# The last four groups' second product of a feed-forward layer, from full products to seven half-wide block products

## The chip, the cores and the metric

The kernel runs on one core of a Trainium2 chip (trn2). TensorE (PE) multiplies and loads weights (PEld), VectorE (DVE) and ScalarE (ACT) do elementwise work, GpSimd (POOL) issues indirect transfers, SyncE (SP) issues the other DMAs. The metric is the device time of one execution in microseconds.

## The reference

```python
def reference(q, k, v, g_norm, moe..., moe2...):
    kv = einsum('bhsd,bhse->bhde', k, v);  o = einsum('bhsd,bhde->bhse', q, kv)
    o = o / sqrt(mean(o * o) + 1e-06) * g_norm        # (8, 8, 576, 64)
    x = o.transpose(0, 2, 1, 3).reshape(4608, 512)
    # tokens with x @ w_skip > 0 go to one of 8 experts (512 -> 1024 -> 512, relu), others stay
    x[e] = x[e] + gate * (maximum(x[e] @ w1[e], 0) @ w2[e])
    h = x @ w_in                                       # second feed-forward: (4608, 2048)
    return (h * sigmoid(h)) @ w_out                    # (4608, 512)
```

All is float32. The change lies in the last line, for a part of the tokens.

## The kernel before

Every float32 product is made of three fast ones: each operand is split into a high part (ACT, a copy that rounds) and a low part (DVE, the difference), and PE adds high x high, high x low and low x high. After attention and the experts, the second feed-forward runs over nine groups of 512 tokens, each in four tiles of 128 (`s`). Three groups are *dense*: in 16 steps a step makes 128 hidden columns (`first`) and multiplies the step before's by `w_out` (`second`). The other six groups go in three *pairs*, one `super_group(k)` each, k = 0, 1, 2; here they are called pair one, two and three. A pair's two groups are the two halves of one axis, and its first product is done in seven block products instead of eight (a Strassen-Winograd scheme).

A pair has two stages. The **block stage** calls `block(q)` 56 times: six matmuls of 512 columns each (`pa`, `pb`, `pc` in PSUM), then a sum on DVE and the activation on ACT write a quarter of a hidden tile `g` (`hidden_of(j)`, j = 0 to 7, each with two parts `fi` of the hidden axis for two groups `ni`). The **product stage** runs 32 steps `x`: `prepare(x + LEAD)` makes the two parts `h` of a quarter of `g`, four steps ahead (ACT, then DVE, five buffers `h` in turn), and `product(x)` multiplies it by a part of `w_out`, twelve matmuls of 512 columns into `acc`. All eight PSUM banks hold the eight output tiles; the last step's results are copied out by ACT and DVE in turn and stored (`finish_group`). The last block of the block stage is called after step 0.

The weights of a pair come from DRAM as *entries* of 1 MB into a ring of five tiles (`NWE`): 14 with four blocks each (`weights_a`) and 8 of `w_out` (`weights_b`). `load_entry` asks for the entry five places on when the last product that reads an entry has been issued; SP's queue holds these loads, the stores and everything else it issues in program order. The plain parts are written to DRAM during dense group two (`keep_part`), the sums of the weights of the first product later (`sums_of`).

The next pair's tokens are gathered by POOL (`fetch_pair`, eight calls of four indirect DMAs, held back by `pace`, a copy that waits for a piece of `g`), turned by DVE, summed and split into the seven block operands `b0` to `b6` (`operand_parts`, in the product stage of the pair before). The order is written out by hand: Python generators are stepped once a block or step, and each engine runs its instructions in that order.

## Time and profile before

| | us |
|---|---|
| three runs | 1158.49, 1159.91, 1160.99 |
| median | 1159.91 |
| the profiled execution | 1158.88 |
| its span | 1157.1 |
| PE busy | 1122.7 (97%) |
| DVE busy | 601.7 (52%) |
| ACT busy | 501.8 (43%) |

Three views are read. The table of stages gives the busy time of each engine in a stretch of time. The timeline gives the start of a run of like instructions, the time to the end of its last, and how many there are; the distance between two starts divided by the count is the time that one takes from its neighbours. The chain gives what ended last, step by step.

### The profile page before, as it was taken

How to read it: one execution, taken by the hardware profiler on the slowest of the kernel's cores; microseconds unless marked ns; L12 is line 12 of the kernel's file. 1: busy time of each engine (PE TensorE's matmuls, PEld its weight loads, DVE VectorE, ACT ScalarE, POOL GpSimd, SP SyncE). 2: the span in 40 equal slices, each digit the busy share in tenths (PEclk: the TensorE clock that was granted, in tenths of full speed). 3: DMA queues.
4: the chain of work that ended last, by engine and by line, in shares of the span. 5: the costliest groups of instructions: out<-in, count | busy, mean ns of one | idle time of the engine just before them, and what ended most of it. 6: DMA issues, size and time to landing. Idle time of an engine off the chain costs nothing.

```text
span 1157.1 us, 16746 instructions
## 1 busy us (share of the span) xinstructions
PE 1122.7 (97%) x6283; PEld 934.5 (81%) x6283; DVE 601.7 (52%) x1111; ACT 501.8 (43%) x983; POOL 324.2 (28%) x337
## 2 busy tenths in 40 slices
PE   8994699999999999999999999999999999999998
PEld 7884698888888888788888888888888888888886
DVE  2468578888887599533535422454122554223222
ACT  3675355555554555433333444432344332344221
POOL 3689224323331174150145043200142300000000
PEclk9998799999999999999999999999999999999999
DMA  9996557666666433198351676422666423654202
GB/s 341 365 359 241 192 165 234 215 223 211 220 208 201 153 120 122 45 292 263 122 161 35 205 262 211 162 105 78 227 220 214 140 73 141 219 187 172 89 31 73
DMA packets 65267, 211.07 MB, mean 182 GB/s; under 512 B 9840, under 2 KB 24688, under 8 KB 53024
## 3 DMA queue, kind: packets, MB, share of 16 engines
q1 hardware_dynamic: 55760, 189.44, 46.8%
q0 software_dynamic: 8064, 20.48, 6.0%
q8 instruction: 50, 0.82, 0.3%
q10 hardware_dynamic: 1360, 0.05, 0.1%
q14 instruction: 33, 0.27, 0.1%
HBM read 162.67 MB, written 47.27 MB: 181 GB/s over the span
## 4 chain that ended last, share of the span: by engine, by line
PE 90%; DVE 4%; DMA 3%; ACT 2%; issue 1%; POOL 0%; SPq 0%; DVEq 0%; ACTq 0%
PE acc L1526 23%; PE acc L1383 21%; PE ph L1331 20%; PE pa L1479 11%; PE pc L1479 6%; PE pb L1479 3%; PE po L474 2%; PE kv L442 1%; PE pt L1232 1%; DMA q<-in_q_dram 1%; DMA v<-in_v_dram 1%; DVE x L217 1%; PE busy L1148 1%; PE kv L444 0%; DVE x L199 0%
## 5 line engine op out<-in xcount | busy, mean ns | idle before, releaser
L1383 PE MATMUL acc<-w,h 128*128 128x512 f32 x1128 | 277.3, 392 | 0.5 <-ACT h L1344 0.5
L1526 PE MATMUL acc<-entry,h 128*128 128x512 f32 x1152 | 265.1, 392 | 0.0
L1331 PE MATMUL ph<-xT,w 128*128 128x512 f32 (+7 forms) x1344 | 264.3, 345 | 0.5 <-ACT xT L1243 0.3
L1526 PEld LDWEIGHTS acc<-entry,h 128*128 128x128 f32 x1152 | 216.3, 188 | 47.9
L1331 PEld LDWEIGHTS ph<-xT,w 128*128 128x128 f32 x1344 | 223.7, 188 | 30.2 <-ACT xT L1243 0.5
L1383 PEld LDWEIGHTS acc<-w,h 128*128 128x128 f32 x1128 | 201.0, 181 | 48.0 <-ACT h L1344 1.0
L1022 POOL DMA_INDIRECT x<-xs,qidx x128 | 128.5, 1004 | 110.8 <-DVE room L1294 48.8
L1507 DVE TENSOR_TENSOR h<-g,h 128x512 fp32r<-128x512 f32 x96 | 66.5, 693 | 147.9 <-ACT h L1506 147.9
L1479 PE MATMUL pa<-b,entry 128*128 128x512 f32 x576 | 141.8, 393 | 0.0
L1479 PEld LDWEIGHTS pa<-b,entry 128*128 128x128 f32 x576 | 108.2, 188 | 24.8
L1506 ACT ACTIVATE h<-g 128x512 fp32r<-128x512 f32 x96 | 60.5, 630 | 146.6 <-PE acc L1526 146.6
L188 DVE TENSOR_TENSOR w<-stg_None,w 128x1024 fp32r<-128x1024 f32 x64 | 83.9, 1312 | 17.3 <-ACT w L187 17.1
L1461 ACT ACTIVATE g<-g 128x512 f32<-128x512 f32 x72 | 45.4, 633 | 103.3 <-DVE g L1459 103.3
L1345 DVE TENSOR_TENSOR h<-sg,h 128x512 fp32r<-128x512 f32 x48 | 33.1, 691 | 96.3 <-ACT h L1344 96.3
L222 POOL TENSOR_TENSOR x<-x,x 128x512 f32<-128x512 f32 x32 | 56.1, 1753 | 96.4 <-DVE x L209 96.2
L1343 ACT ACTIVATE sg<-ph 128x512 f32<-128x512 f32 x48 | 28.7, 597 | 111.3 <-PE ph L1331 111.1
L187 ACT ACTIVATE w<-stg_None 128x1024 fp32r<-128x1024 f32 x64 | 67.4, 1054 | 17.6 <-DMA xs<-rows 9.5
L1479 PE MATMUL pc<-b,entry 128*128 128x512 f32 x288 | 74.3, 393 | 0.0
L1337 ACT ACTIVATE h<-ph 128x304 fp32r<-128x304 f32 (+6 forms) x64 | 27.9, 436 | 97.0 <-PE ph L1331 95.2
L1479 PEld LDWEIGHTS pc<-b,entry 128*128 128x128 f32 x288 | 54.1, 188 | 12.4
L1459 DVE TENSOR_TENSOR g<-pc,u 128x512 f32<-128x512 f32 x24 | 16.6, 691 | 73.0 <-PE pc L1479 73.0
L629 POOL TENSOR_TENSOR rows<-rows,grow 128x512 f32<-128x512 f32 x36 | 41.7, 1186 | 31.9 <-ACT rows L487 31.9
(219 smaller groups left out, 1151.9 us busy)
## 6 DMA issues: line engine op xcount, KB each, us to landing
entry<-wa SPq DMA_DIRECT2D x42, 1024.0 KB, 4.9
stg_None<-in_we_dram SPq DMA_DIRECT2D x64, 512.0 KB, 3.9
entry<-wb SPq DMA_DIRECT2D x24, 1024.0 KB, 4.8
stg<-in_wf_dram SPq DMA_DIRECT2D x32, 512.0 KB, 4.1
xs<-rows SPq DMA_DIRECT2D x8, 1032.0 KB, 9.6
wb<-w SPq DMA_DIRECT2D x16, 512.0 KB, 5.0
wa<-parts SPq DMA_DIRECT2D x32, 256.0 KB, 4.1
k<-in_k_dram SPq DMA_DIRECT2D x7, 1024.0 KB, 8.8
```

The lines of the kernel that those rows point to most:

```text
L187: nc.scalar.activation(w[:, 0, :], t.bitcast(F32), AF.Copy)
L188: nc.vector.tensor_tensor(w[:, 1, :], t.bitcast(F32), w[:, 0, :].bitcast(F32), ALU.subtract)
L222: nc.gpsimd.tensor_tensor(x3, x3, x2, ALU.mult)
L629: nc.gpsimd.tensor_tensor(xv, xv, f.to_broadcast([P, HP, 2, D]), ALU.mult)
L1022: nc.gpsimd.indirect_dma_start(out=rows_of[u][s][:, a * XQ:(a + 1) * XQ], out_offset=None, in_=xblocks, in_offset=bass.IndirectOffsetOnAxi ...
L1331: nc.tensor.matmul(ph[:, 0:n], w[:, wi, kk * P:(kk + 1) * P], x[:, xi, 0:n], start=(kk == 0 and a == 0), stop=(kk == KD - 1 and a == 2),)
L1383: nc.tensor.matmul(accs[u, s][0:m], h[:, hi, s * P:s * P + m], w[:, wi, DM:2 * DM], start=(f == 0 and a == 0), stop=(last and a == 2),)
L1461: nc.scalar.activation(g, acc, AF.Silu)
L1479: nc.tensor.matmul(p, w[:, wi, kk], x[:, xi, kk], start=(i in FIRST_IN_BANK and kk == 0 and a == 0), stop=(kk == 1 and a == 2), skip_group ...
L1506: nc.scalar.activation(h[:, 0], g, AF.Copy)
L1507: nc.vector.tensor_tensor(h[:, 1], g, h[:, 0].bitcast(F32), ALU.subtract)
L1526: nc.tensor.matmul(acc[ni, s], h[:, hi, s * P:(s + 1) * P], w[:, wi], start=(j == 0 and fi == 0 and a == 0), stop=(last and a == 2),)
```

## The change

For pairs two and three the second product is done as seven block products too, and the eight quarters of `w_out` and of `g` are combined for it. One block product takes eight steps, `product_second(x)`, of twelve matmuls with 256 columns; 56 steps make a pair's product stage. `SECOND` is the order of the block products and `PLACE` the quarter of `g` that each reads. `third_sum` (in the block stage) and `later_sum` (in the product stage, 24 calls from step 12 on, three in four steps) overwrite quarters of `g` with sums. The results of the block products gather in two PSUM tiles each (`two`), are summed on the way out into `t`, `v` and `z`, and are stored by halves of the columns (`put_half`).

The sums of `w_out` are made once, in pair one's product stage, from the entries that it reads (`sums2_of`, one call for each of the eight), and stored in DRAM (`weights_t`, eight 128 KB stores for each call); a pair's entries for the product are then 14 instead of 8. `weights_b` is one DRAM tile with the two column halves apart, so that pair one's product reads its moving operand in two pieces.

The operands of the next pair are summed in the block stage (`operand_sums`, at blocks 18, 26, 34 and 42), written to DRAM (two stores of 512 KB a tile), read again (`load_sums`) and only split in the product stage (`operand_split`). The gathers come at blocks 3, 7, ... 31 instead of 6, 13, ... 41 and two in the product stage.

```diff
-    weights_b = [tc.dram_tile([P, 2, 2 * DM], F32, name=f"wb{j}") for j in range(KJ)]
+    weights_b = tc.dram_tile([P, KJ, 2, 2 * DM], F32, name="wb")
+    JH = KJ // 2
+    weights_t = {(i, h): tc.dram_tile([P, JH, DM], F32, name=f"wt{i}_{h}") for i in (4, 5, 6, 7) for h in range(2)}
+    tokens_ab = {}
+    SECOND = (1, 4, 2, 6, 5, 7, 3)
+    PLACE = {1: (0, 0), 4: (1, 1), 2: (1, 0), 6: (1, 1), 5: (0, 0), 7: (0, 1), 3: (1, 0)}
+    COLUMNS = {1: (0, 0), 2: (1, 0), 3: (1, 1)}
...
-            nc.sync.dma_start(weights_b[j][:, odd].rearrange("p (o d) -> p o d", o=2), w[:, :, DM:2 * DM])
+            for h in range(2):
+                a = DM + h * EH
+                nc.sync.dma_start(
+                    weights_b[:, j, odd, h * DM:(h + 1) * DM].rearrange("p (o d) -> p o d", o=2), w[:, :, a:a + EH]
+                )
...
+    def sums2_of(j, w):
+        vec = nc.vector
+        even, odd, s12, high = (xp.tile([P, DM], F32, tag="x", name=nm) for nm in ("even", "odd", "s12", "high"))
+        for t, o in ((even, 0), (odd, 1)):
+            wo = w[:, o].bitcast(F32).rearrange("p (h o d) -> p o h d", h=2, o=2)
+            vec.tensor_tensor(t.rearrange("p (h d) -> p h d", h=2), wo[:, 0], wo[:, 1], ALU.add)
...
+        (b11, b12), (b21, b22) = ((t[:, 0:EH], t[:, EH:DM]) for t in (even, odd))
+        t1, t2, t3, t4 = s12[:, 0:EH], s12[:, EH:DM], b11, b12
+        for o, x, y in ((t1, b12, b11), (t2, b22, t1), (t3, b22, b12), (t4, b21, t2)):
+            vec.tensor_tensor(o, x, y, ALU.subtract)
+        yield
+        for hi, t, ab in ((odd, s12, (5, 6)), (high, even, (7, 4))):
+            nc.scalar.activation(hi.bitcast(F32R), t, AF.Copy)
+            vec.tensor_tensor(t.bitcast(F32R), t, hi, ALU.subtract)
+            for h, i in enumerate(ab):
+                e, slot = divmod(j, JH)
+                for o, part_ in enumerate((hi, t)):
+                    nc.sync.dma_start(
+                        weights_t[i, e][:, slot, o * EH:(o + 1) * EH], part_[:, h * EH:(h + 1) * EH]
+                    )
+            if t is s12:
+                yield
...
+    def operand_sums(u, s):
+        vec = nc.vector
+        ab, sums = (stg.tile([P, 2 * DM], I32, tag="stg", name=nm).bitcast(F32) for nm in ("ab", "sums"))
+        ta, tb, t12, t34 = ab[:, 0:DM], ab[:, DM:2 * DM], sums[:, 0:DM], sums[:, DM:2 * DM]
+        for v, t in ((u, ta), (u + 1, tb)):
+            vec.transpose(t.rearrange("p (k a i) -> p a k i", k=KD, a=KQ), x_of(rows_of[v][s]))
...
+        vec.tensor_tensor(t1, b12, b11, ALU.subtract)
+        vec.tensor_tensor(t2, b22, t1, ALU.subtract)
+        yield
+        vec.tensor_tensor(t3, b22, b12, ALU.subtract)
+        vec.tensor_tensor(t4, b21, t2, ALU.subtract)
+        kept_ab, kept_t = (tc.dram_tile([P, 2 * DM], F32, name=f"{nm}{u}_{s}") for nm in ("ab", "st"))
+        nc.sync.dma_start(kept_ab, ab)
+        nc.sync.dma_start(kept_t, sums)
+        tokens_ab[u, s] = kept_ab, kept_t
+        yield
...
+    def load_sums(u, s):
+        kept_ab, kept_t = tokens_ab.pop((u, s))
+        if s % 2 == 0:
+            loaded["b22"] = sgp.tile([P, GN], F32, tag="sg", name="b22")
+        t = [xgp.tile([P, XW], F32, tag="xg", name="sums")[:, 0:DM] for _ in range(3)]
+        b22 = loaded["b22"][:, s % 2 * EH:(s % 2 + 1) * EH]
+        nc.sync.dma_start(t[0], kept_ab[:, 0:DM])
+        nc.sync.dma_start(b22, kept_ab[:, 2 * DM - EH:2 * DM])
+        for i in range(2):
+            nc.sync.dma_start(t[1 + i], kept_t[:, i * DM:(i + 1) * DM])
...
+        for ii in ((0, 1, 2), (4, 5), (6, 3), ()):
+            for i in ii:
+                nc.scalar.activation(at(i, 0), views[i], AF.Copy)
+            for i in old:
+                nc.vector.tensor_tensor(at(i, 1), views[i], at(i, 0).bitcast(F32), ALU.subtract)
+            old = ii
+            if ii:
+                yield
...
-    entries = ([("a", e) for e in range(NEA)] + [("b", j) for j in range(KJ)]) * NSUP
+    entries, entry0 = [], []
+    for k in range(NSUP):
+        entry0.append(len(entries))
+        entries += [("a", e) for e in range(NEA)]
+        entries += [("b", j) for j in range(KJ)] if k == 0 else [("c", (i, h)) for i in SECOND for h in range(2)]
...
+        if kind == "c" and i[0] in COLUMNS:
+            odd, h = COLUMNS[i[0]]
+            src = weights_b[:, i[1] * JH:(i[1] + 1) * JH, odd, h * DM:(h + 1) * DM]
+            nc.sync.dma_start(t.rearrange("p (j d) -> p j d", j=JH), src)
+            return
+        src = weights_b[:, i] if kind == "b" else weights_a[i] if kind == "a" else weights_t[i]
+        nc.sync.dma_start(t, src.rearrange("p a b -> p (a b)"))
...
+            w = ring[e0 + NEA + j][:, fi].rearrange("p (h o d) -> p o h d", h=2, o=2)
...
+                        acc[ni, s].rearrange("p (h d) -> p h d", h=2), h[:, hi, s * P:(s + 1) * P], w[:, wi],
...
+        def third_sum(j):
+            g = hidden_of(j)
+            nc.vector.tensor_tensor(g[:, 0, 1], g[:, 0, 0], g[:, 0, 1], ALU.subtract)
+        def later_sum(n):
+            i, j = divmod(n, KJ)
+            g = hidden_of(j)
+            o, x, y, op = (
+                (g[:, 1, 1], g[:, 1, 1], g[:, 0, 1], ALU.subtract),
+                (g[:, 0, 0], g[:, 1, 1], g[:, 0, 0], ALU.add),
+                (g[:, 1, 0], g[:, 1, 0], g[:, 1, 1], ALU.subtract),
+            )[i]
+            nc.vector.tensor_tensor(o, x, y, op)
...
+            g = hidden_of(j)[(slice(None),) + PLACE[SECOND[i]]]
+            h = ready[x] = next_h()
+            nc.scalar.activation(h[:, 0], g, AF.Copy)
+            nc.vector.tensor_tensor(h[:, 1], g, h[:, 0].bitcast(F32), ALU.subtract)
...
+        def product_second(x):
+            n, j = divmod(x, KJ)
+            i = SECOND[n]
+            if j == 0 and i in (1, 4, 6, 5):
+                two[i] = [
+                    ps_a.tile([P, DM], F32, tag=f"a{m + 2 * (i == 5)}", name="two") if i in (1, 5)
+                    else ps_h.tile([P, GN], F32, tag="h", name="two") if i == 4
+                    else ps_t.tile([P, GN], F32, tag="t", name="two") for m in range(2)
+                ]
+            p = two[{2: 1, 7: 6, 3: 5}.get(i, i)]
...
+            last = j == KJ - 1
+            for s in range(GT):
+                for a, (hi, wi) in enumerate(((0, 0), (0, 1), (1, 0))):
+                    nc.tensor.matmul(
+                        p[s // 2][:, s % 2 * EH:(s % 2 + 1) * EH], h[:, hi, s * P:(s + 1) * P], w[:, wi],
+                        start=(i in (1, 4, 6, 5) and j == 0 and s % 2 == 0 and a == 0), stop=(last and a == 2),
+                        skip_group_check=True,
+                    )
+            if slot == 3:
+                load_entry(e0 + NEA + e + NWE)
+            if not last:
+                return
...
+            if i == 1:
+                for m, t in enumerate(pair_of("t")):
+                    nc.scalar.activation(t, p[m], AF.Copy)
+            elif i == 2:
+                for m in range(2):
+                    o = xgp.tile([P, XW], F32, tag="xg", name="o")[:, 0:DM]
+                    nc.scalar.activation(o, p[m], AF.Copy)
+                    put_half(0, m, o, 0)
+            elif i in (4, 6):
+                for m, t in enumerate(pair_of({4: "v", 6: "z"}[i])):
+                    vec.tensor_tensor(t, p[m], keeps["t"][m], ALU.add)
+            elif i == 5:
+                for m, t in enumerate(keeps["t"]):
+                    vec.tensor_tensor(t, p[m], t, ALU.add)
+            else:
+                for nm, ni, h in ((("z", 0, 1),) if i == 3 else (("v", 1, 0), ("t", 1, 1))):
+                    for m, t in enumerate(keeps.pop(nm)):
+                        vec.tensor_tensor(t, p[m], t, ALU.add)
+                        put_half(ni, m, t, h)
...
         for q in range(NB - 1):
             block(q)
-            j, x = divmod(q, 7)
-            if more_ and j < 6 and x == 6:
-                pace(hidden_of(j)[:, 0, 1])
-                fetch_pair(j // 2, j % 2)
+            for j in new:
+                third_sum(j)
+            i, j = blocks_order[q]
+            new = [j] if i == 1 and k > 0 else []
+            if more_:
+                n, x = divmod(q - 3, 4)
+                if x == 0 and 0 <= n < 2 * GT:
+                    if n:
+                        pace(recent[0])
+                    fetch_pair(n // 2, n % 2)
+                n, x = divmod(q - 18, 8)
+                if x == 0 and 0 <= n < GT:
+                    turning.append(operand_sums(u + 2, n))
+                step_on(turning)
+                if q in (49, 51):
+                    load_sums(u + 2, (q - 49) // 2)
             if q >= NB - 1 - 3 * LEAD and (NB - 1 - q) % 3 == 0:
-                prepare(LEAD - (NB - 1 - q) // 3)
-            yield
-        for x in range(4 * KJ):
-            prepare(x + LEAD)
-            product(x)
+                (prepare_second if k else prepare)(LEAD - (NB - 1 - q) // 3)
+            yield
...
+        SPLIT_AT = {0: 0, 4: 1, 8: 2, 48: 3} if k else {2: 0, 8: 1, 14: 2, 20: 3}
+        for x in range((7 if k else 4) * KJ):
+            if k:
+                if x == 1:
+                    for j in new:
+                        third_sum(j)
+                n0, n1 = (max(0, min(3 * KJ, -(-3 * (y - 12) // 4))) for y in (x, x + 1))
+                for n in range(n0, n1):
+                    later_sum(n)
+                prepare_second(x + LEAD)
+                product_second(x)
+            else:
+                prepare(x + LEAD)
+                product(x)
             if x == 0:
                 block(NB - 1)
             if more_:
-                s, p = divmod(x - 2, 6)
-                if p == 0 and 0 <= s < GT:
-                    room = [xp.tile([P, DM], F32, tag="x", name="room") for _ in range(4)]
-                    queue.append(operand_parts(u + 2, s, room))
+                if x in SPLIT_AT:
+                    queue.append(operand_split(u + 2, SPLIT_AT[x]))
                 if queue and next(queue[0], queue) is queue:
                     queue.pop(0)
-                if x in (5, 6):
-                    fetch_pair(GT - 1, x - 5)
-            yield
+                if x - 4 in SPLIT_AT and SPLIT_AT[x - 4] + 2 < GT:
+                    load_sums(u + 2, SPLIT_AT[x - 4] + 2)
+            if k == 0:
+                if x % 4 == 0:
+                    sums_now.append(sums2_of(x // 4, ring[e0 + NEA + x // 4]))
+                step_on(sums_now)
+            yield
```

On PE, around the last block of pair two's block stage (`pa`, `pb` are its blocks, `entry` the weights). Before:

```order
L1479 MATMUL pb<-b_7533,entry_8458 128x512 x6
L1526 MATMUL acc<-entry_8493,h 128x512 x12
L1479 MATMUL pa<-b_7535,entry_8458 128x512 x6
L1526 MATMUL acc<-entry_8493,h 128x512 x36
L1526 MATMUL acc<-entry_8534,h 128x512 x48
```

and now:

```order
L1595 MATMUL pb<-b_7630,entry_8738 128x512 x6
L1707 MATMUL two<-entry_8782,h 128x256 x12
L1595 MATMUL pa<-b_7632,entry_8738 128x512 x6
L1707 MATMUL two<-entry_8782,h 128x256 x36
L1707 MATMUL two<-entry_8822,h 128x256 x48
```

Behind the same block, runs of twelve with 512 columns have become runs of twelve with 256; from here to the next pair 56 of them stand where 32 stood.

On DVE, in pair two's product stage (`h` is the prepared operand, `g` the hidden tile, `room`, `sums` and `b` belong to the next pair). Before, from step 3 on:

```order
L1507 TENSOR_TENSOR h_8687<-g1_1_8207,h_8687 128x512
L1294 STREAM_TRANSPOSE room_8706<-x15_0_8169 128x4x4x32
L1294 STREAM_TRANSPOSE room_8707<-x16_0_8172 128x4x4x32
L1507 TENSOR_TENSOR h_8719<-g1_1_8207,h_8719 128x512
L1311 TENSOR_TENSOR room_8708<-room_8707,room_8706 128x256
L1312 TENSOR_TENSOR room_8708<-room_8707,room_8708 128x256
L1313 TENSOR_TENSOR room_8709<-room_8707 128x256
L1314 TENSOR_TENSOR room_8709<-room_8706,room_8708 128x256
L1507 TENSOR_TENSOR h_8743<-g1_2_8275,h_8743 128x512
L1308 TENSOR_TENSOR b0_8710<-room_8706,b0_8710 128x2x128
```

and now, at steps 11 to 15:

```order
L1677 TENSOR_TENSOR h_9206<-g1_7_8934,h_9206 128x512
L1411 TENSOR_TENSOR b6_8989<-sums_9073,b6_8989 128x2x128
L1411 TENSOR_TENSOR b3_8986<-sums_9073,b3_8986 128x2x128
L1668 TENSOR_TENSOR g1_0_8369<-g1_0_8369 128x512
L1677 TENSOR_TENSOR h_9226<-g1_0_8369,h_9226 128x512
L1668 TENSOR_TENSOR g1_1_8444<-g1_1_8444 128x512
L1677 TENSOR_TENSOR h_9242<-g1_1_8444,h_9242 128x512
L1668 TENSOR_TENSOR g1_2_8520<-g1_2_8520 128x512
L1677 TENSOR_TENSOR h_9258<-g1_2_8520,h_9258 128x512
L1677 TENSOR_TENSOR h_9273<-g1_3_8608,h_9273 128x512
L1727 TENSOR_TENSOR v_9290<-two_9143,t_9134 128x512
```

Transposes and sums of the next operand have left this stage; beside each low part `h` there now stands a sum over `g`, and from step 15 sums out of PSUM (`v`).

On SP, towards the end of pair two's block stage (`wa`, `wb`, `wt` are weights in DRAM, `ab` and `st` the kept sums). Before:

```order
L1416 DMA entry32_8337<-wa10_88 128x2048
L1416 DMA entry33_8374<-wa11_89 128x2048
L1416 DMA entry34_8414<-wa12_90 128x2048
L1416 DMA entry35_8458<-wa13_91 128x2048
L1416 DMA entry36_8493<-wb0_92 128x2048
L1416 DMA entry37_8534<-wb1_93 128x2048
```

and now:

```order
L1524 DMA entry34_8692<-wa12_90 128x2048
L1524 DMA entry35_8738<-wa13_91 128x2048
L1374 DMA ab15_2_8753<-ab_8725 128x1024
L1375 DMA st15_2_8754<-sums_8726 128x1024
L1521 DMA entry36_8782<-wb_92 128x4x512
L1521 DMA entry37_8822<-wb_92 128x4x512
L1374 DMA ab15_3_8839<-ab_8810 128x1024
L1375 DMA st15_3_8840<-sums_8811 128x1024
L1524 DMA entry38_8872<-wt4_0_93 128x2048
L1387 DMA sums_8893<-ab15_0_8566 128x512
```

Between the loads of entries there now stand the stores of the kept sums and the loads that bring them back.

## Rows read from the trace of the kernel before

**Rows 1.** The page: busy us by engine; PE, its clock, DMA by slice.

```profile
PE 1122.7 (97%) x6283; PEld 934.5 (81%) x6283; DVE 601.7 (52%) x1111; ACT 501.8 (43%) x983; POOL 324.2 (28%) x337
...
PE   8994699999999999999999999999999999999998
...
PEclk9998799999999999999999999999999999999999
...
GB/s 341 365 359 241 192 165 234 215 223 211 220 208 201 153 120 122 45 292 263 122 161 35 205 262 211 162 105 78 227 220 214 140 73 141 219 187 172 89 31 73
```

**Rows 2.** The page: the chain that ended last, by engine.

```profile
PE 90%; DVE 4%; DMA 3%; ACT 2%; issue 1%; POOL 0%; SPq 0%; DVEq 0%; ACTq 0%
```

**Rows 3.** Stages: block, product of pairs one, two, three; columns in the first line.

```profile
core 0: us, PE busy (x) PEld busy (x) DVE busy (x) ACT busy (x) POOL busy (x), PEclk, DMA share, GB/s
655.50:734.50 79.00, 79.00 (x344) 64.27 (x343) 20.73 (x31) 36.67 (x61) 23.90 (x30) 1.00 0.66 227
734.50:821.20 86.70, 86.70 (x380) 71.00 (x379) 41.25 (x83) 28.39 (x60) 7.81 (x8) 1.00 0.33 116
821.20:900.10 78.90, 78.90 (x343) 64.20 (x342) 19.95 (x30) 36.11 (x61) 23.90 (x30) 1.00 0.65 220
900.10:986.50 86.40, 86.40 (x380) 70.98 (x379) 41.25 (x83) 28.40 (x60) 8.72 (x8) 1.00 0.33 116
986.50:1065.40 78.90, 78.90 (x344) 64.29 (x343) 20.10 (x30) 36.11 (x61) 0.00 (x0) 1.00 0.56 200
1065.40:1152.40 87.00, 87.00 (x379) 70.75 (x377) 21.15 (x31) 19.84 (x32) 0.00 (x0) 1.00 0.17 63
```

**Rows 4.** Timeline of PE around step 0: start us, us, instruction, count.

```profile
897.36 2.92 PE L1526 MATMUL acc<-entry,h 128*128 128x512 f32 x12
900.12 1.53 PE L1479 MATMUL pa<-b,entry 128*128 128x512 f32 x6
...
1062.59 2.92 PE L1526 MATMUL acc<-entry,h 128*128 128x512 f32 x12
1065.35 1.56 PE L1479 MATMUL pa<-b,entry 128*128 128x512 f32 x6
```

**Rows 5.** The chain in order of time, from 655 us: start us, us.

```profile
826.95 2.80 PE pa L1479 x12
...
901.65 85.00 PE acc L1526 x372
1066.92 85.60 PE acc L1526 x372
```

**Rows 6.** Timeline of PE in the last expert and a dense group.

```profile
374.41 1.60 PE L1331 MATMUL ph<-xT,w 128*128 128x256 f32 x12
375.85 1.55 PE L1383 MATMUL acc<-w,h 128*128 128x512 f32 x6
377.24 1.58 PE L1331 MATMUL ph<-xT,w 128*128 128x256 f32 x12
378.65 1.55 PE L1383 MATMUL acc<-w,h 128*128 128x512 f32 x6
...
388.09 1.04 PE L1232 MATMUL pt<-ident,sorted 128*128 128x128 f32 x8
388.88 1.63 PE L1383 MATMUL acc<-w,h 128*128 128x512 f32 x6
...
402.62 2.88 PE L1383 MATMUL acc<-w,h 128*128 128x512 f32 x12
405.34 2.88 PE L1331 MATMUL ph<-xT,w 128*128 128x512 f32 x12
```

**Rows 7.** Groups by shape, whole span: busy us, mean ns, idle before.

```profile
L1331 PE MATMUL ph<-xT,w 128*128 128x256 f32 x96 | 12.7, 282 | 0.0
...
L1526 PEld LDWEIGHTS acc<-entry,h 128*128 128x128 f32 x1152 | 216.3, 188 | 47.9
```

**Rows 8.** Groups by shape in the three pairs, 655 us to the end.

```profile
L1507 DVE TENSOR_TENSOR h<-g,h 128x512 fp32r<-128x512 f32 x96 | 66.5, 693 | 147.9 <-ACT h L1506 147.9
L1308 DVE TENSOR_TENSOR b<-room,b 128x256 fp32r<-128x256 f32 x56 | 20.1, 418 | 0.0
...
L1294 DVE STREAM_TRANSPOSE room<-x 128x512 f32<-128x512 f32 x16 | 10.4, 687 | 0.0
...
L1506 ACT ACTIVATE h<-g 128x512 fp32r<-128x512 f32 x96 | 60.5, 630 | 146.6 <-PE acc L1526 146.6
...
L1304 ACT ACTIVATE b<-room 128x256 fp32r<-128x256 f32 x56 | 18.7, 402 | 0.0
...
L1022 POOL DMA_INDIRECT x<-xs,qidx x64 | 62.2, 972 | 70.4 <-DVE room L1294 48.8 <-issue 19.8 <-DMA entry<-wa 1.1
```

**Rows 9.** Timeline of DVE: two runs of splits in pair one.

```profile
745.78 1.09 DVE L1308 TENSOR_TENSOR b<-room,b 128x256 fp32r<-128x256 f32 x3
...
748.57 1.46 DVE L1308 TENSOR_TENSOR b<-room,b 128x256 fp32r<-128x256 f32 x4
```

**Rows 10.** The page: DMA issues, count, KB each, us to landing.

```profile
entry<-wa SPq DMA_DIRECT2D x42, 1024.0 KB, 4.9
```

**Rows 11.** Waits of SP's queue from 655 us: total us, times, longest.

```profile
SPq L1416 <- PE acc L1526: 180.8, 19, 10.7
```

**Rows 12.** Timeline of the end: a load's issue, the last copy, the last stores.

```profile
1097.50 0.32 SPq L1416 DMA_DIRECT2D entry<-wb  x1
...
1152.54 0.69 DVE L1356 COPY o<-acc 128x512 f32<-128x512 f32 x1 [0.67 <-PE acc L1526]
1153.26 1.11 SPq L1371 DMA_DIRECT2D out_dram<-o  x2
```

More of the change, by code (lines that the diff above doesn't have):

```diff
@@ new lines, in operand_split, with at @@
+    def operand_split(u, s):
+        if s == 0:
+            operand_tiles()
+        src = loaded.pop((u, s))
+        def at(i, o):
+            return operands[i][:, o, :, s * P:(s + 1) * P]
+        views = {i: x.rearrange("p (k n) -> p k n", k=2) for i, x in src.items()}
+        old = ()
+        for ii in ((0, 1, 2), (4, 5), (6, 3), ()):
[6 more added lines that the diff above has]
+                yield
@@ L1370, in finish_group @@
                 t0 = (2 * bp + h) * S + SM
-                nc.sync.dma_start(out[t0:t0 + SR, :], o[h * SR:(h + 1) * SR, :])
+                nc.sync.dma_start(out[t0:t0 + SR, a:z], o[h * SR:(h + 1) * SR, :])
     def second(u, f, c, h):
@@ L1429, in next_h, with step_on @@
         return stg.tile([P, 2 * DM], I32, tag="stg", name="h").bitcast(F32R).rearrange("p (o n) -> p o n", o=2)
+    def step_on(queue):
+        if queue and next(queue[0], queue) is queue:
+            queue.pop(0)
     def super_group(k):
@@ L1581, in tile_kernel @@
     hs = {}
-    sums_now = []
     parts = []
     rooms = []
-    def step_on(queue):
-        if queue and next(queue[0], queue) is queue:
-            queue.pop(0)
     for n in range(len(steps) + LAG):
```

48 lines of the change are left out of this document (40 added, 8 removed).

## The prediction

> **What bounds the kernel now.** First the page: PE is busy 97% of the span and in nearly all of the 40 slices, with its clock at 9 tenths or more in all but two of them [rows 1], and the chain that ended last is 90% PE [rows 2]. So I ask which engine could take PE's place in the part that is edited. The table by stages answers [rows 3]. From 655 us on there are three pairs of groups, each with a block stage (56 block products of six matmuls) and a product stage (32 steps of twelve matmuls). In all six PE is busy without a gap at granted clock 1.00 (2.4 GHz), while DVE is busy 20 to 41 us of 79 to 87, ACT 20 to 37, and the DMA engines 17 to 66%. PE's queue never runs dry there, so the time of a stage is the number of its matmuls times the distance between their starts. That distance I take from starts, not from busy time, because neighbours overlap.
>
> **Removed: the second product of pairs two and three.** Pair two: twelve matmuls from 897.36 to 900.12 (2.76 us) and 372 that hold the chain for 85.00 us, together 87.8. Pair three: 2.76 and 85.60, together 88.4 [rows 4, 5]. Sum 176.1 us.
>
> **Added in its place.** Seven block products of eight steps are 56 steps of twelve matmuls, with 256 columns instead of 512. This shape stands in the trace: the last expert's first product has bursts of twelve 128x256 matmuls on the same kind of operands, between bursts of six with 512 columns. Twelve narrow ones take 374.41 to 375.85 and 377.24 to 378.65, that is 1.44 and 1.41 us; six wide ones between them take 1.39 [rows 6]. I take 1.425 us a step: 56 x 1.425 = 79.8 us a pair, 159.6 for two. **Gain 176.1 - 159.6 = 16.5 us.** The ends: 1.41 a step gives 157.9 (gain 18.2), 1.44 gives 161.3 (gain 14.8). A much worse end is the busy time of the 96 narrow ones, 12.7 us, or 132 ns each [rows 7]; it counts the run-on of every burst, so I don't take it, but it is a rival below. Narrower does not keep paying: eight matmuls of 128 columns begin at 388.09 and the next burst at 388.88, about 100 ns each [rows 6], against 118 for 256 columns, so 256 lies just above a floor that has little to do with columns.
>
> Here a rule speaks. The Trainium skill ("TensorE: Matmul & The Clock Gate", section "LDWEIGHTS (loading the stationary operand)") puts a load of 128 columns at 128/1.2 = 107 ns, whatever the matmul's width, which speaks against halving widths; its section "Back-to-back issue gap" gives 262 cycles for 256 columns, 109 ns at 2.4 GHz. By those figures, as an estimate, two pairs would take 147 us and the time would be 1131. The trace has about 119 and decides.
>
> **DVE and ACT in pair two** (the tightest place). A step now lasts 1.43 us, before 2.7. Each step needs one high part on ACT (0.63) and one low part on DVE (0.69) of the next operand; twenty-four later sums and twelve sums out of PSUM cost 0.69 each on DVE, a split of 256 columns 0.40 on ACT and 0.42 on DVE, seven for each of four tiles [rows 8]. Steps 0 to 11: 12 x 0.69 + 21 x 0.42 + 0.69 = 17.8 us on DVE against 12 x 1.43 + 1.4 (the last block) = 18.5 on PE; where splits follow each other they take 1.09 for three and 1.46 for four [rows 9], which makes it 16.6. Steps 12 to 43: 1.75 x 0.69 = 1.21 a step, with six PSUM sums 42.8 us against 45.6. ACT: 12 x 0.63 + 21 x 0.40 = 16.0 of 18.5. All under PE's time, and operands are made four steps (5.7 us) ahead, while one takes 0.63 + 0.69 once its buffer is free. I put 0 here, and no gain, since none of it shortens PE's work. What is late next if the cover fails: PE's matmuls of the next step. Bound: if DVE loses 0.3 us a step to waits for ACT while it is this full, 1.51 stands against 1.43 for 32 steps (2.6 us) and the first twelve steps end 2 late (16.6 + 3.6 against 18.5): 4.6 us. Pair three has no splits, and DVE work of 56 x 0.69 + 24 x 0.69 + 12 x 0.69 = 63 us of 80.
>
> **DVE and ACT elsewhere.** Transposes and sums of the next operands move from the product stages into the block stages of pairs one and two: 4 x (2 x 0.69 + 4 x 0.42) = 12.2 us onto a DVE that is busy 20 of 79 [rows 3, 8], with 5.5 for the eight third sums of pairs two and three. Pair one's product stage gains, for each of eight weight tiles, 4 x 0.69 + 4 x 0.42 = 4.4 us on DVE, 35.5 in all, and 10 on ACT: DVE goes from 41 to about 65 of 87 with the move taken off, in steps of 2.7 us. Hidden. The gathers on POOL come at every fourth block (5.6 us) instead of every seventh; four of them at 0.97 and about 0.3 of issue are 5.1 [rows 8], and the first sums wait for them only at block 18. Hidden.
>
> **DMA and SP's queue.** A block stage that also fetches moved 220 GB/s at a share of 0.65, so all engines busy would be about 338 [rows 3]. Pairs one and two add there 4.2 MB of kept sums, 1.8 of reloads, 0.5 of gathers: 6.5 MB in 79 us, 303 GB/s, a share of 0.90; between blocks 18 and 46 nearly 1. Product stages rise to about 230 (pair one, 8.4 MB of weight sums in 64 stores), 221 and 150. Cover: an entry of weights is asked for when its slot is freed, four entries ahead (4 x 5.6 = 22 us), and lands in 4.9 [rows 10]; SP waits for PE at these loads, 181 us in the largest of four groups [rows 11], so it has time to issue. 17 us of lateness are free. A store waits for DVE in SP's queue with the next entries behind it, some 3 us, inside those 17. The keeping of plain weights in dense group two takes 16 more stores, about 0.32 us of SP each [rows 12], 5 us over a group of 87: 0.
>
> **Small terms.** Pair one's product now reads its moving operand in two pieces. No row shows that; equal-width matmuls differ from 227 ns (twelve in 2.72 in a dense group [rows 6]) to 230 (372 in 85.60) and 233 (twelve of a block stage in 2.80) [rows 5], so I bound it by -1 and +1.5 and take +0.5. The end: today a copy of 0.69 and two stores follow the last matmul, 4.6 us to the end [rows 12]; then a sum of 0.69 and two half-wide stores. +0.3, between -0.3 and +0.7.
>
> **Sum.** The profiled execution took 1158.9 us (span 1157.1 and 1.8 around it): 1158.9 - 16.5 + 0.5 + 0.3 = 1143.2. The median of three runs lies 1.0 above it, so 1144.
>
> **Rivals.** (a) *DVE late in pair two*: worked out above, 4.6 us, with the other small ends up to 8: 1147 to 1152. For it: 90 to 95% of DVE's time is planned away over 44 steps, with work that waits for PSUM in order. Against: four steps of lead.
> (b) *No fixed part at all*: if a narrow matmul cost half of the dense group's 227, 113 ns, two pairs would take 152 and the time would be about 1137. Against: the narrow bursts themselves [rows 6]. The Trainium skill's figures above go this way and further.
> (c) *Weight loads show*: at the 132 ns of busy time a pair takes 672 x 0.132 = 88.7, hardly more than before, and the time is 1160 to 1162: the change does nothing. A weight load takes 188 ns [rows 7] and hides only behind its neighbours; from 131 ns a matmul nothing is gained. Against: the bursts of twelve hid it [rows 6].
> (d) *Slower, by DMA in the block stages of pairs one and two*: if stores, gathers and loads together got no more than today's 220 GB/s, 23.9 MB would take 109 us, less the stage's 79 and the 17 of cover 12 us each, 24 in all: 1168. It decides from about 230 GB/s downwards. Against: 292 and over 340 stand in slices of this trace [rows 1].
>
> **How the numbers follow.** Forecast 1141 to 1147: 0.66. (a) 0.19, (b) 0.06, (c) 0.04, (d) 0.05. Likeliest time 1144. For eight in ten I take in (a) up to 1151 and the fringe of (b) from 1140.5; (c), (d) and the rest of (b) stay outside. A measurement tells about 0.2% (2.3 us) from no change: faster 0.91, same 0.04, slower 0.05.
>
> **What would show it.** Right: 1344 narrow matmuls about 119 ns apart, PE without gaps through pairs two and three at 1.00, product stages of some 80 us, block stages still 79, the DMA share near 0.9 there. Wrong: idle time of PE ended by DVE or ACT between steps 0 and 48 of pair two (a), by an entry's DMA (d); narrow matmuls over 125 ns apart (c); a product stage of pair one over 88 us (the two-piece read).

## The result and the profile after

The changed kernel took 1146.24 us (median of four, 1142.78 to 1147.48) against 1159.22 us: 0.9877, with a 95% interval of 0.986 to 0.9893, 13 us faster. The profiled execution is the fastest of the four, 1142.78 us, span 1141.0. On two more chips the ratio was 0.9853 (0.983 to 0.9875) and 0.9889 (0.9869 to 0.9909).

The two traces, stage by stage, from the start of each stage's first matmul (for pair one the first behind the last dense product, since two of its blocks run earlier; the last row from the start of the last matmul):

| stage | before, us | after, us | difference |
|---|---|---|---|
| up to pair one | 658.22 | 657.80 | -0.42 |
| block stage, pair one | 73.53 | 73.53 | 0.00 |
| product stage, pair one | 89.44 | 89.44 | 0.00 |
| block stage, pair two | 76.16 | 78.02 | +1.86 |
| product stage, pair two | 89.13 | 80.65 | -8.48 |
| block stage, pair three | 76.10 | 76.28 | +0.18 |
| product stage, pair three | 89.52 | 80.44 | -9.08 |
| from the last matmul on | 4.97 | 4.86 | -0.11 |
| span | 1157.1 | 1141.0 | -16.1 |

The page of the changed kernel (busy us by engine, then slices), beside [rows 1]:

```profile
PE 1104.5 (97%) x6859; PEld 947.4 (83%) x6859; DVE 712.9 (62%) x1303; ACT 537.8 (47%) x1047; POOL 327.1 (29%) x339
...
PEclk9998799999999999999999999999999999999999
DMA  9996657666666534087541479859789875755561
```

PE holds 97% as before, and DVE has 111 us more work. The table of stages, beside [rows 3] (block, product of pairs one, two, three):

```profile
core 0: us, PE busy (x) PEld busy (x) DVE busy (x) ACT busy (x) POOL busy (x), PEclk, DMA share, GB/s
657.80:731.30 73.50, 73.50 (x319) 59.78 (x318) 29.13 (x51) 33.23 (x56) 28.14 (x35) 1.00 0.89 301
731.30:820.80 89.50, 89.50 (x392) 73.28 (x391) 62.55 (x125) 37.67 (x78) 0.47 (x1) 1.00 0.73 229
820.80:898.80 78.00, 76.61 (x332) 61.79 (x331) 33.88 (x59) 34.59 (x59) 32.37 (x39) 1.00 0.91 304
898.80:979.40 80.60, 80.60 (x679) 80.34 (x678) 66.09 (x119) 44.51 (x87) 0.00 (x0) 1.00 0.72 233
979.40:1055.70 76.30, 76.30 (x332) 62.07 (x331) 23.49 (x36) 33.98 (x57) 0.00 (x0) 1.00 0.60 205
1055.70:1136.30 80.60, 80.60 (x679) 80.25 (x677) 57.68 (x91) 36.67 (x59) 0.00 (x0) 1.00 0.48 151
```

Five of the six stages have PE busy for every moment at granted clock 1.00 (2.4 GHz; 0.50 is 1.2 GHz). The block stage of pair two has not: 76.61 of 78.00. The timeline of PE at its end (start us, us):

```profile
893.16 1.65 PE L1595 MATMUL pa<-b,entry 128*128 128x512 f32 x6 [1.39 <-DVE g L1573]
...
898.79 1.59 PE L1707 MATMUL two<-entry,h 128*128 128x256 f32 x12
900.22 1.55 PE L1595 MATMUL pa<-b,entry 128*128 128x512 f32 x6
```

The chain, in order of time:

```profile
882.76 8.37 DMA ab<-ab
891.12 0.02 issue
891.15 0.64 ACT h L1676
...
891.81 0.45 DVE h L1677
...
901.77 77.83 PE two L1707 x660
```

Two things are in these rows. The narrow matmuls, 660 in 77.83 us, are 117.9 ns apart, and step 0 takes 900.22 - 898.79 = 1.43. And PE's gap (1.39 of the 1.86 us; the rest lies in the matmuls next to it, as the six behind it, 1.65 for 1.40) is followed back through DVE and ACT to a *store*: the kept sums `ab`, issued at 882.76 and landed 8.37 us later. The timelines of ACT and of DVE show who waited (in brackets the idle time before and what ended it). ACT:

```profile
891.15 0.63 ACT L1676 ACTIVATE h<-g 128x512 fp32r<-128x512 f32 x1 [3.96 <-DMA ab<-ab]
```

DVE, behind it:

```profile
891.81 0.69 DVE L1677 TENSOR_TENSOR h<-g,h 128x512 fp32r<-128x512 f32 x1 [5.77 <-ACT h L1676]
892.42 0.68 DVE L1573 TENSOR_TENSOR g<-pa,p 128x512 f32<-128x512 f32 x1
```

The prepared operand `h` goes in turn to two buffers of its own and three of a pool (`stg`) from which `operand_sums` now takes `ab` and `sums` too. The high part of `h` could not be written until the store had read `ab` out. ACT and DVE work in order: the sum that empties `pa` stood behind the low part of `h`, and PE needed the PSUM bank.

### The profile page after: what moved, and what is told of

It is laid out like the page before. It is cut to its first block, busy times and chain, and to the rows that moved or that the text cites. A ratio compares the mean times of both kernels' runs of the same rounds, so it can differ in the third digit from the quotient of the medians.

```text
span 1141.0 us, 18526 instructions
## 1 busy us (share of the span) xinstructions
PE 1104.5 (97%) x6859; PEld 947.4 (83%) x6859; DVE 712.9 (62%) x1303; ACT 537.8 (47%) x1047; POOL 327.1 (29%) x339
## 4 chain that ended last, share of the span: by engine, by line
PE 90%; POOL 3%; DMA 2%; DVE 2%; ACT 1%; issue 1%; SPq 0%; DVEq 0%; ACTq 0%
PE acc L1481 22%; PE ph L1424 20%; PE two L1707 14%; PE pa L1595 11%; PE acc L1642 8%; PE pc L1595 6%; PE pb L1595 3%; POOL rows L664 3%; PE po L509 2%; PE kv L477 1%; PE pt L1267 1%; DMA ab<-ab 1%; DVE x L252 1%; PE kv L479 1%; PE G L498 1%
## 5 line engine op out<-in xcount | busy, mean ns | idle before, releaser
L1707 PEld LDWEIGHTS two<-entry,h 128*128 128x128 f32 x1344 | 159.0, 190 | 0.3
L1707 PE MATMUL two<-entry,h 128*128 128x256 f32 x1344 | 159.1, 281 | 0.0
L1677 DVE TENSOR_TENSOR h<-g,h 128x512 fp32r<-128x512 f32 x112 | 77.0, 691 | 42.6 <-ACT h L1676 40.0
L1676 ACT ACTIVATE h<-g 128x512 fp32r<-128x512 f32 x112 | 70.5, 630 | 68.5 <-PE two L1707 53.1
L1642 PE MATMUL acc<-entry,h 128*128 128x512 f32 x384 | 88.4, 392 | 0.0
L1642 PEld LDWEIGHTS acc<-entry,h 128*128 128x128 f32 x384 | 72.1, 188 | 15.9
```

The costliest lines, as they stand in the source:

```text
L1642: nc.tensor.matmul(acc[ni, s].rearrange("p (h d) -> p h d", h=2), h[:, hi, s * P:(s + 1) * P], w[:, wi], start=(j == 0 and fi == 0 and a = ...
L1676: nc.scalar.activation(h[:, 0], g, AF.Copy)
L1677: nc.vector.tensor_tensor(h[:, 1], g, h[:, 0].bitcast(F32), ALU.subtract)
L1707: nc.tensor.matmul(p[s // 2][:, s % 2 * EH:(s % 2 + 1) * EH], h[:, hi, s * P:(s + 1) * P], w[:, wi], start=(i in (1, 4, 6, 5) and j == 0 a ...
```

## The experiments

Four runs (the first runs with DVE's low part repeated on half and on all steps, the first with three copies, and the quarters) fell on a chip on which the kernel before took 1187.16 us and every kernel lost time in places far from its edit, for a cause that I could not find; of those runs only stretches without such stalls are read, and two of the kernels were run again elsewhere.

### The stall at h: one line

```diff
         recent = [None]
+        hr_n[0] = 0
```

`hr_n` counts the buffers of `h`. Set to zero at the start of a pair, it gives the first two prepared operands of a block stage the buffers of their own; the shared three are then needed some six blocks later. No transfer changes.

The changed kernel again:

> The changed kernel again, for its spread and a second profile. Its profiled run took 1142.8 us, its other three 1145.6 to 1147.5. Theory (h buffer): in a pair's block stage the kept sums (ab, st) and the prepared operand h take turns in the same three buffers, so ACT has to wait for a store to be read out before it can write h; in the profile that wait was 3.96 us and cost PE 1.8 us at 893, and it is longer in the slower runs. Then most runs here take 1145 to 1147.5, and if the new profile falls on such a run, the idle time of PE at the end of pair two's block stage is 3 to 6 us, or one of the same kind stands in pair one (at 730), and the rest of the span agrees within 0.5 us. Rival (clock): the slower runs have the same waits, and the clock that was granted is lower over some stretch, with matmuls in it at over twice their distance. Rival (spread of its own): the runs scatter around 1145 as those of the kernel before scatter, by 2.5 us, with no place in the trace.

With the line:

> The changed kernel with one line added: the count that picks the buffer of h starts at zero in every pair, so that the first two prepared operands go to two buffers of their own and the three that are shared with the kept sums are needed at blocks 49, 52 and 55 and not from 43 on. Transfers, their number and their order stay as they are. Theory (h buffer): the idle time of PE at the end of pair two's block stage (1.8 us in the profile) goes, ACT waits under 1 us for ab or st, and the time is 1140.5 to 1142 in nearly every run, 0.995 to 0.998 of the changed kernel, with a spread under 2 us. Rival (transfers at their limit, share 0.91): the stall stays or moves to an entry of weights, and the time is that of the changed kernel within 0.1%. Rival (clock or scatter): the profiled stall goes, 1.8 us, but the spread of 4 to 5 us stays.

Measured on one chip: changed 1143.64 (1143.03 to 1146.69), with the line 1142.54 (1141.49 to 1147.28); ratios to before 0.9853 (0.983 to 0.9875) and 0.9854 (0.9827 to 0.9882). The medians don't separate them; the traces do. The block stage of pair two took 77.83 us without the line and 76.16 with it, as in the kernel before, and PE has no gap. ACT's timeline there, with the line, has `h` without a wait:

```profile
888.31 0.62 ACT L1677 ACTIVATE h<-g 128x512 fp32r<-128x512 f32 x1
```

The table of that stage, with the line:

```profile
822.30:898.46 76.16, 76.16 (x331) 61.96 (x330) 34.01 (x59) 34.72 (x59) 32.38 (x39) 1.00 0.91 304
```

The DMA share is the same 0.91 as with the stall. So the cause is the shared buffer, and not transfers at their limit. But the theory's second half fell: the spread stayed. The profile of the changed kernel here was its slowest run, 1146.69, with the same gap as the fast one (1.7 us of that stage, not the 3 to 6 expected of a slower run). Its span is 3.9 us longer than that of the 1142.78 run, and 4.1 us were there when pair one began (661.89 against 657.80). 3.3 of them were there by 16 us; the table from 10 to 20 us, of the 1142.78 run:

```profile
10.00:20.00 10.00, 7.10 (x102) 5.95 (x101) 0.55 (x1) 3.20 (x10) 0.00 (x0) 1.00 0.98 383
```

Of this one:

```profile
10.00:20.00 10.00, 6.92 (x84) 5.92 (x82) 0.00 (x0) 1.04 (x3) 0.00 (x0) 0.66 0.98 370
```

PE waited 2.7 us for `v` of attention there, against 1.0, and its granted clock was 0.66 against 1.00. The edit isn't near. That the start makes the scatter is shown for this one run only.

Both kernels once more, on a third chip:

> The changed kernel once more beside the one with h's buffers in the new order, for the ratio of the two on another chip. On the chip of the first pair the changed kernel's block stage of pair two lost 1.7 to 1.8 us at one place (893 to 897) and the runs scattered by 4 us over the first 15 us of the span, where the inputs of attention land. Theory: the same here, block stage of pair two 77.6 to 78.0, pairs' product stages 79.2; the time 1143 to 1147. Rival (the stall at h belongs to that chip): 75.9.

> The changed kernel with h's buffers in the new order, again beside the changed kernel. Theory: block stage of pair two 75.9 and everything after it the same to 0.1 us, the median 1.5 to 2 us under that of the changed kernel, within the scatter of the start. Rival (the gain was chance): medians within 0.5 us.

Measured: 1147.18 (1143.28 to 1150.25; 0.9889, 0.9869 to 0.9909) and 1143.25 (1142.07 to 1144.64; 0.9851, 0.9834 to 0.9868). Block stage of pair two: 77.88 with ACT's wait of 4.13 us for `ab`, and 76.16 without. The profiled spans differ by 1.2 us (1141.5 and 1140.3): this stage makes 1.7, and the start 0.4 the other way. The median's 3.9 us are more than the trace explains. The version with the line is the fastest of this study.

### The price of width

The kernel before, with second products in halves, and then in quarters (4 for 2, `P` for `EH`):

```diff
-                for a, (hi, wi) in enumerate(((0, 0), (0, 1), (1, 0))):
+                for z in range(2):
+                    for a, (hi, wi) in enumerate(((0, 0), (0, 1), (1, 0))):
...
-                        acc[ni, s], h[:, hi, s * P:(s + 1) * P], w[:, wi],
+                        acc[ni, s][:, z * EH:(z + 1) * EH], h[:, hi, s * P:(s + 1) * P],
+                        w[:, wi, z * EH:(z + 1) * EH],
...
```

> The kernel before, with every second product of the three pairs issued as 256-column halves: 24 matmuls a step in place of 12, with the same columns, the same products and no other change (768 narrow ones a pair in place of 384 wide). It measures the price of width alone. Theory (118 to 119 ns for a narrow one, 230 for a wide one): a pair's product takes 768 x 0.1185 = 91.0 in place of 88.3 us, 2.7 more a pair, 8 in all: 1166 to 1168. Rival (no fixed part, 113 to 115 ns): 768 x 0.114 = 87.6, 0 to -2 in all: 1157 to 1160. Rival (weight loads show, 132 ns): 768 x 0.132 = 101.4, 39 in all: 1198. Rival (the operand does not change from half to half... it does here, each half loads its three operands again; if a repeated order of high, high, low is what hides the loads, 118 stays).

Measured: 1168.8 us (1166.28 to 1171.10), 1.0072 of before (1.0047 to 1.0098), some 9 us longer. Pair one in the chain:

```profile
734.28 2.87 PE acc L1527 x24
...
738.56 87.83 PE acc L1527 x744
```

744 in 87.83 us are 118.05 ns each, and the pair's product stage took 92.10 us for 89.44. The three product stages lost 2.66, 2.80 and 2.18 us, 7.6 in all, so the theory's 8 holds; 2.4 more stood ahead of pair one. The same columns in halves cost 3% more, so what the change gains comes from the multiplications saved (56 x 12 x 256 columns for 32 x 12 x 512, an eighth less), and 3% of the stage goes back for the width.

> The kernel before with every second product of the pairs issued as 128-column quarters, 48 matmuls a step (1536 a pair). With halves a narrow one took 118 ns in the long run (744 in 87.8 us) against 229 for a wide one. Theory (a floor of about 100 ns a matmul that columns do not lower, as eight of 128 columns showed in 0.79 us): 1536 x 0.100 = 154 us a pair, +64, 192 in all: about 1350. Rival (a fixed part of some 7 to 11 ns beside the columns, no floor): 1536 x 0.062 = 95 a pair, +6: 1178. Rival (weight loads of 188 ns of busy time show in full): 289 a pair, +200: 1760.

Measured: 1711.34 us, far above the theory, and near the last rival's 1760 for another reason than the rival's. The table of stretches, three of pair one's product and one of pair three's, shows two prices:

```profile
755.00:770.00 15.00, 15.00 (x130) 14.72 (x129) 4.49 (x8) 3.50 (x6) 0.50 (x1) 1.00 0.22 74
770.00:800.00 30.00, 28.12 (x169) 27.77 (x169) 5.86 (x14) 4.12 (x11) 7.19 (x8) 0.69 0.17 53
800.00:900.00 100.00, 100.00 (x471) 100.00 (x471) 14.56 (x29) 9.29 (x20) 0.00 (x0) 0.50 0.06 22
...
1539.00:1600.00 61.00, 61.00 (x549) 61.00 (x547) 8.31 (x12) 7.95 (x13) 0.00 (x0) 1.00 0.16 57
```

At granted clock 1.00 one takes 61.00 / 549 = 111 ns, at 0.50 (1.2 GHz) 100 / 471 = 212. So in this stream there is a floor, at 111 and not at 100, and 118 for 256 columns lies 6% above it; pair three, at 1.00 throughout, took 172.8 us for 89.5, 83 more where the theory had 64. The Trainium skill ("TensorE: Matmul & The Clock Gate", section "LDWEIGHTS (loading the stationary operand)") puts a load at its columns divided by 1.2, 107 ns for 128 columns, and 111 agrees with that to 4%. That the loads make the floor is not shown. That the clock fell to half in pairs one and two I had not foreseen, and it makes the larger part of the miss. In pair one PE was busy without a pause for 16 us at 1.00, then paused four times for 0.2 to 0.8 us (in pair two three times for 0.4 to 0.8), and from there to the end of the stage it stood at 0.50, though it was busy all the time; in pair three, without the pauses, it stayed at 1.00. Pauses alone are not enough: the product stages with 256 columns of the run with every low part made twice (below) stood at 1.00 through 50 waits of PE of up to 1.7 us. What else is needed is open, and so is whether that chip had a part in it: the quarters ran on no other.

### The cover of the transfers

An unused copy inside DRAM at each of the eight sums of operands, with the one line above; then three.

```diff
         nc.sync.dma_start(kept_ab, ab)
         nc.sync.dma_start(kept_t, sums)
+        nc.sync.dma_start(tc.dram_tile([P, 4, DM], F32, name=f"more{u}_{s}"), weights_a[s])
```

> The kernel with h's buffers in the new order, and one unused copy of 1 MB inside DRAM (from the kept weights to a scratch tile) at each of the eight sums of the next operands: 4 MB read and 4 MB written more in the block stages of pairs one and two, where the DMA share is 0.86 to 0.91. It measures the cover of the transfers, which the prediction put at 17 us a stage, and the rival that transfers bind. At some 340 GB/s with all engines busy a stage of 79 us can move 26.9 MB; it would have 24 + 4 (a copy counted once) or + 8 (counted twice). Theory (cover of 17 us): 28 to 32 MB need 82 to 94 us, 3 to 15 late, inside the cover but for what h and the reloads wait: 0 to 4 us a stage, 1140 to 1149. Rival (no cover: what is late shows): 3 to 15 us a stage, 1147 to 1171, with PE idle for entries in pairs one and two.

Measured: 1144.13 us (1143.81 to 1146.55), 0.9861 (0.9834 to 0.9888), against 1142.54 without the copies on that chip. The profiled runs differ by 1.8 us, of which 1.5 stand ahead of pair one and 0.3 in pair two's product stage. The two block stages:

```profile
660.00:735.00 75.00, 75.00 (x326) 60.99 (x325) 30.13 (x54) 33.73 (x56) 28.16 (x35) 1.00 0.93 332
824.00:900.00 76.00, 76.00 (x331) 61.80 (x330) 34.13 (x59) 34.54 (x58) 32.80 (x39) 1.00 0.96 339
```

339 GB/s at a share of 0.96, and PE has no gap: what didn't fit went into the product stage (257 GB/s for 238 in pair two). The cover is there, and rival (d) is far off.

> The kernel with h's buffers in the new order and three unused 1 MB copies inside DRAM at each of the eight sums of the next operands (12.6 MB a pair, counted once, in pairs one and two). With one copy each, the block stages moved 332 and 339 GB/s at shares of 0.93 and 0.96, and PE had no gap: what did not fit moved into the product stage. Theory (the prediction's cover of some 17 us, at 340 GB/s): 24 + 12.6 = 36.6 MB a stage need 108 us, 29 late against 17 of cover: 8 to 16 us a pair, with PE idle for entries from about block 44 on or early in the product stage; 1157 to 1173. Rival (cover is larger, since copies queue behind one another on their own and entries share the engines with them rather than wait behind them): 0 to 4 a pair, 1141 to 1149. Rival (no cover): 29 a pair, 1199.

> The run with three unused 1 MB copies at each sum of operands again: its first run fell on a chip where the kernel before took 1187 us and all kernels lost time at places that have nothing to do with the copies, so that its block stages can't be read. Theory (cover of some 17 us at 340 GB/s): 36.6 MB need 108 us, 29 late, 8 to 16 us a pair. Rival (entries share the engines with the copies and the cover is larger): 0 to 4 a pair, 1141 to 1149. In the first run only 2.6 us of PE's waits were put down to an entry, which speaks for the rival.

The first of these took 1220.09 us on the chip of 1187.16, and its block stages aren't read; its product stages, 96.9 and 94.3 us, agree with the second's 96.6 and 94.7. The second took 1190.58 us: 11.4 and 7.1 us more than the kernel with the line in pair one's two stages, 10.9 and 14.2 in pair two's. That is 18.5 and 25.1 a pair, above the theory's 8 to 16, far above the one rival's 4 and under the other's 29. But the theory named the wrong cover. Waits of PE (total us, times, longest):

```profile
PE pa L1598 <- ACT t L1571: 10.6, 4, 5.6
PE acc L1645 <- DVE g L1576: 4.9, 1, 4.9
PE pa L1598 <- DVE g L1576: 4.7, 1, 4.7
PE pc L1598 <- DMA entry<-wa: 4.2, 2, 2.7
PE two L1710 <- ACT h L1679: 3.5, 1, 3.5
```

Waits of DVE:

```profile
DVE sums L1368 <- DMA ab<-ab: 27.8, 4, 10.5
```

The page's landings (count, KB, median us):

```profile
entry<-wa SPq DMA_DIRECT2D x42, 1024.0 KB, 5.9
ab<-ab SPq DMA_DIRECT2D x8, 512.0 KB, 17.6
```

PE waited 28 us in all, and the ring of entries lost 4.2 of them. What ran out first were the three shared buffers: their stores landed after 17.6 us (8.6 in the changed kernel), DVE waited 27.8 us for room for the next sums, and PE waited for the ACT and DVE work behind that. ACT's splits waited another 15.8 us for the reloads (`sums<-ab`). The other 15 of the 43.6 us stand in stages whose granted clock was 0.93 to 0.96, where the kernel with the line had 1.00.

### How near DVE is to its limit

The low part of `h` made twice in pairs two and three, on even steps or on all, with the one line above:

```diff
-            nc.vector.tensor_tensor(h[:, 1], g, h[:, 0].bitcast(F32), ALU.subtract)
+            for _ in range(1 + (x % 2 == 0)):
+                nc.vector.tensor_tensor(h[:, 1], g, h[:, 0].bitcast(F32), ALU.subtract)
```

> The kernel with h's buffers in the new order, and on every second step of pairs two and three DVE makes the low part of h twice (the same result again). It asks how near DVE is to becoming the bound there. In the trace of the changed kernel DVE's operations on 512 columns are busy for 0.69 us but start 0.60 apart when nothing holds them. Theory (spacing counts): steps 12 to 43 need 1.75 x 0.60 + 0.11 for sums out of PSUM = 1.16 us of DVE a step, with the half repeat 1.46, against 1.42 of PE: 1.3 us late after 32 steps, inside the four steps of lead. So 0 to 0.5 us a pair, product stages of 79 to 80, as without it. Rival (busy time counts, as the prediction's bound for a late DVE had it): 1.75 x 0.69 + 0.13 + 0.345 = 1.68 a step, 8.4 us late after 32 steps, less 4 to 5 of lead: 3 to 5 us a pair, product stages of 82 to 84.

> The run with DVE's low part made twice on every second step again, for pair two, whose block stage was disturbed in the first run: its product stage took 82.0 us, pair three's 79.6, against 79.2 and 79.2 without the repeats. A repeat took 0.73 us there, since it writes the same tile as the operation ahead of it. Theory (pair two is nearer to DVE's limit by its splits in steps 0 to 11 and has no lead left at step 12): 81 to 82 again in pair two, 79.4 to 79.7 in pair three. Rival (the disturbed start of that stage): 79.3 to 79.7 in both.

The first run gave 1195.53 us on the chip of 1187.16, the second 1153.36. The expectations mix two ways of counting; counted alike, the 660 matmuls behind the last block took 82.0 us in pair two and 78.1 in pair three in both runs, against 77.7 and 77.8 without repeats. So pair two's 4.3 us do not come from that chip. They lie in the first rival's 3 to 5 and not in the theory's 0 to 0.5; pair three's 0.35, for 0.72 us more of DVE in every two steps, fits the theory alone. What the two pairs differ by are the splits: in the second run DVE was busy for 22.5 of the first 24.4 us of pair two's product stage and for 19.8 of pair three's, and in pair two PE's waits for `h` begin right behind these 24.4 us.

> The same with the low part made twice on every step of pairs two and three. Theory (spacing counts): 1.16 + 0.60 = 1.76 us of DVE a step against 1.42 of PE, 11 us late after 32 steps, less 4 to 5 of lead: 6 to 8 us a pair, product stages of 85 to 88, with PE waiting for h by DVE from about step 25 on; in pair two 2 to 4 more for the splits of steps 0 to 11 (17 spaced operations more). Rival (busy time counts): 2.03 a step, 19.6 late, less 5: 15 us a pair, 95. Rival (DVE's work is hidden in any case, since PE's queue is long): 0, 79.

Measured 1229.73 us on the chip of 1187.16; the product stages, free of its stalls, took 103.6 and 94.9 us, 23.1 and 14.3 more than without repeats: far more than the theory's 8 to 12 and 6 to 8, and in pair three near the rival's 15. A part of the reason is in the timeline of DVE; first the changed kernel (start, us to the end of the last, count):

```profile
919.88 0.69 DVE L1668 TENSOR_TENSOR g<-g 128x512 f32<-128x512 f32 x1
920.48 0.69 DVE L1677 TENSOR_TENSOR h<-g,h 128x512 fp32r<-128x512 f32 x1
921.08 0.69 DVE L1668 TENSOR_TENSOR g<-g 128x512 f32<-128x512 f32 x1
```

With the repeats:

```profile
1150.49 1.41 DVE L1679 TENSOR_TENSOR h<-g,h 128x512 fp32r<-128x512 f32 x2
1151.82 0.68 DVE L1669 TENSOR_TENSOR g<-g 128x512 f32<-128x512 f32 x1
```

Operations on different tiles start 0.60 apart though each is busy for 0.69; the repeat, on the tile just written, starts 1.41 - 0.69 = 0.72 after the first. With it a step needs 1.16 + 0.72 = 1.88 us of DVE against 1.42, which makes 15 over 32 steps. I had priced the repeat too low. But less the 4 to 5 of lead that is 10 to 11, and what makes the rest of pair three's 14.3 is open. So the totals don't tell the theory from the rival; the steps do. Two that PE waited for in pair three:

```profile
1165.46 1.68 PE L1709 MATMUL two<-entry,h 128*128 128x256 f32 x12 [0.25 <-DVE h L1679]
1167.39 1.69 PE L1709 MATMUL two<-entry,h 128*128 128x256 f32 x12 [0.25 <-DVE h L1679]
```

They start 1.93 apart, which is DVE's spacing of a low part, its repeat and a sum, 0.60 + 0.72 + 0.61; three times 0.69 would be 2.07.

## Why the prediction was right, and where it was not

**What bounds the kernel.** Right: PE without gaps at 1.00 in five of six stages, so number times distance was the time.

**Narrow steps.** Right, a little dear: 1.425 us a step forecast from two bursts, 1.415 measured (117.9 ns). The two product stages together lost 17.6 us for 16.5. (b) and (c) are out: without waits the sustained runs at 256 columns stand 117.7 to 118.1 ns apart, not 113 and not 132. The Trainium skill's 262 cycles ("TensorE: Matmul & The Clock Gate", section "Back-to-back issue gap"), as an estimate 109 ns at 2.4 GHz, are given there for an isolated gap and lie 8% under the trace's 118.

**Two-piece read.** +0.5 taken, 0.00 measured; the chain before and after:

```profile
736.06 85.30 PE acc L1526 x372
735.63 85.30 PE acc L1642 x372
```

The 89.44 us of this product stage are not the prediction's sign of a dear read (over 88): they are counted from step 0 on and were the same before. **The end.** +0.3 taken, -0.11 measured.

**DVE in pair two, rival (a).** 0 taken, and no wait of PE for DVE stands in the product stages. My pricing by 0.69 us an operation was too dear: DVE was busy for 15.4 us in the time of steps 0 to 11 and 40.3 in that of steps 12 to 43, where I had 16.6 to 17.8 and 42.8. The bound was not: in the repeats some 0.36 us a step more cost pair two 4.3 us, near the 4.6 that I had put on 0.3 a step, and pair three 0.35. So in pair two rival (a) was less than one operation every other step away.

**DMA, rival (d).** 303 GB/s at a share of 0.90 forecast for the block stages, 301 and 304 at 0.89 and 0.91 measured; an entry landed in 5.9 us for 4.9 [rows 10] without PE noticing. 4 MB more a pair cost 0.3 us. The 17 us of cover were worked out for the entries alone, and with 12.6 MB more the shared buffers gave out before them.

**What failed: the step on the stores.** I costed a store as a wait of SP's queue, "some 3 us, inside those 17", and let it end there. I did not ask who needs the buffer that it reads. `h` takes it in turn, and at a share of 0.91 the store landed in 8.4 us. That is the +1.86 in the block stage of pair two, shown by the one line that removes it. Terms too dear by 1.1 (steps), 0.5 and 0.4, and 0.4 ahead of pair one, against 1.86 and 0.18 missed: so the profiled 1142.8 came out beside the 1143.2 of the sum, partly by errors that cancel.

**Profile and median.** I put the median 1 us above the profiled run; it lay 3.5 above, at 1146.24, and the medians on two more chips were 1143.64 and 1147.18, the last outside my range of 1141 to 1147. So that the first median fell inside it was in part luck: the sum speaks of the profiled run. The run of 1146.69 lost its 4.1 us ahead of pair one, most of it in the start of attention. The five executions of the changed kernel up to 1143.64 us show a mean granted clock of 0.989, the nine from 1144.96 on 0.982 to 0.987; which of the two, time or clock, follows from the other no run here shows. For the rest the cause is open, and so is why the changed kernel scatters up to 1150.25 and, with the line, only to 1147.28.

## What to carry to other kernels

Where PE never waits, price a change by the distance between starts that the same shape has elsewhere in the trace, as here, where the sustained runs bore it out to a per cent. When a change adds a store, cost not only its queue but the buffer that it reads: list who takes that buffer next, and what stands behind that engine's wait in its order. And price DVE's load by the spacing of its operations, not by their busy time, and look up the spacing for the same order of tiles.

## What the runs showed of the hardware that I had not expected

- 128x128x128 matmuls, each with its weight load, run 111 ns apart at granted clock 1.00; in two of three stages, after three or four pauses of up to 0.8 us, the clock stood at 0.50 for the rest of the stage, in which PE was busy 100%, and each took 212 ns. With 256 columns two stages kept 1.00 through 50 waits of up to 1.7 us.
- DVE's 128x512 operations are busy for 0.69 us and start 0.60 apart on different tiles, 0.72 on the tile just written.
- Two chips ran the kernel before in 1159.5 and 1160.0 us, a third in 1187.16 (one run); what it lost there is open.
